# Early queries and keys in wide pieces, transposed head by head on TensorE, and strided values in four transfers per pair

## The chip, the cores and the metric

The kernel runs on one core of one Trainium2 chip. The metric is the device time of one execution in microseconds (us); lower is better. The core has five engines that work side by side and meet by semaphores: TensorE (PE; PEld is its loading of stationary tiles), VectorE (DVE), ScalarE (ACT), GpSimd (POOL) and SyncE (SP), which here only issues transfers. Each engine runs its own list of instructions strictly in order, so an instruction that waits holds up all that stand behind it. "SPq" and "ACTq" in the profile are the issue of transfers by SP and ACT.

## The reference

Eight batches of attention with 8 heads, 576 positions and 64 columns per head, followed by a gated feed-forward product of 4608 tokens. The first four heads see a local window of 32 positions, the other four only positions that are equal modulo 32.

```python
scores = scale * np.matmul(q, k.transpose(0, 1, 3, 2))
rel = pos[:, None] - pos[None, :]
mask_local = (rel >= 0) & (rel < stride)
mask_strided = (rel >= 0) & (pos[None, :] % stride == pos[:, None] % stride)
masks = np.stack([mask_local if h < H // 2 else mask_strided for h in range(H)], axis=0)
scores = np.where(masks[None, :, :, :], scores, -1000000000.0)
attn = softmax(scores)
x = np.matmul(attn, v).transpose(0, 2, 1, 3).reshape(B * S, H * D)
h = x @ w_in
g = h * np.clip(h + 3.0, 0.0, 6.0) / 6.0
out = g @ w_out
```

The softmax is written out in the reference (maximum, exponential, sum with 1e-9 added). All inputs are float32; `w_in` is 512 x 2048, `w_out` 2048 x 512.

## The kernel before

**Tiling.** Heads are worked in pairs, so a batch has four pairs: 0 and 1 are local, 2 and 3 strided. Pair numbers stand in the tile names (`qn_2` is the loaded query of a pair 2, `kn_2` its keys, `v_2` its values). The feed-forward part works on tiles of 512 tokens, one per batch, and on the 64 tokens that are left over of each batch, collected over four batches. A tile makes 16 chunks of `w_in` (`ph`, lines 969 to 971: three matmuls with split operands), gates them (`u` on ACT and DVE, `gh` on ACT, `gl` on POOL) and adds each chunk's product with `w_out` to `acc` (lines 927 to 929). Weights are loaded as raw words (`rawi`, `rawo`, line 287), taken apart on ACT, joined on DVE (`fi`, `fo`, line 303) and split into a high and a low part on ACT or POOL (lines 309 to 315). So DVE, ACT and POOL prepare weights and attention while PE multiplies.

**Pairs.** The first eight pairs (batches 0 and 1) go through `kept_pair`, the rest through `pair`. In `kept_pair` the four pairs of batch 0 are "early": their queries and keys come as rows with positions on the partitions (line 454, by SP, for the second pair to start by ACT's queue, two transfers per tensor), PE transposes them against an identity (line 461) into PSUM, and ACT or DVE copies the result to `qplain`, `kplain`, `qt` or `kt` (lines 473 and 475). The strided pairs of batch 1 are loaded by `load_qk` (line 360, four transfers) and transposed by DVE (line 492). Then come scores (`ps`, lines 551 and 554), the softmax in `e`, its transposition on DVE (`atloc` line 632, `atkept` line 637), the product with the values (`pv`, lines 379 and 689), and the high and low part of the result, `x` and `left` (lines 396 and 399), which the feed-forward tile reads. Strided values are loaded by line 511: for each of the two heads four transfers, one for each residue of the position modulo 4.

**Order.** Nothing is ordered by hand. `Plan.emit` is a list scheduler: each operation has an engine, an estimated time, a due time, what it reads and writes, and, for transfers, a time to land; the scheduler simulates the engines with these numbers and emits the instructions in the order that comes out. So a changed estimate can move instructions on every engine. Where PE would be idle ahead of the first products, the plan fills in matmuls of the identity (`idle`, line 1075), one per 0.22 us of planned idle time. Transfers of SP and ACT share eight semaphores in turn: each transfer waits until the one eight places earlier has landed.

Of the kernel before, what the change touches and what calls it, by code (L numbers as in the profile page):

```python
# [10 lines left out]
F32 = mybir.dt.float32  # L11
# [8 lines left out]
P = 128  # L20
# [145 lines left out]
def attention_ffn(ctx: ExitStack, tc, q, k, v, w_in, w_out, out):  # L166
# [241 lines left out]
    def kept_pair(g):  # L408
# [33 lines left out]
        for x in "qk":  # L442
# [6 lines left out]
            if early:  # L449

                def load(x=x, nkey=nkey):
                    t = new(wp, nkey, [P, NQB, 2, D], F32, f"{x}n{nm}")
                    for j in range(2):
                        (nc.scalar if g == 1 else nc.sync).dma_start(
                            t[:QB, :, j], {"q": q, "k": k}[x][b, h0 + j].rearrange("(i p) d -> p i d", p=QB))
                tb = [slot(early) for _ in range(2)]

                def tr(x=x, nkey=nkey, tb=tb):
                    ps = [psum(tb[h], f"{x}p{nm}{h}") for h in range(2)]
                    for i in range(NQB):  # L460
                        nc.tensor.transpose(ps[i // 3][:, i % 3 * QB:i % 3 * QB + QB],
                                            tiles[nkey][:QB, i].rearrange("p j d -> p (j d)"), tiles["ident",][:QB, :QB])

                def evac(e, x=x, tb=tb, h=0):
                    ps, to, half = tiles[tb[h].key][:, :S // 2], qk_of(x), NPOS // 2
                    if loc:
                        c0 = (PAD if x == "k" else 0) + S // 2 * h
                        to = to[:, c0:c0 + S // 2]
                    else:
                        to = to.rearrange("c (r m) -> c m r", r=STRIDE)[:, half * h:half * h + half]  # L470
                        ps = ps.rearrange("c (m r) -> c m r", r=STRIDE)
                    if e == "ACT":
                        nc.scalar.copy(to, ps)
                    else:
                        nc.vector.tensor_copy(to, ps)
                op("ACT" if g == 1 else "SP", 1.06, load, writes=[nkey], due=-60 + 2 * g + (x == "k") - 900 * (g == 1), after=0.9)
                op("PE", 0.13 * NQB * slow, tr, reads=[("ident",), nkey, "plain", tkey[x]], writes=tb, take=tb, due=due - 1020, mode="s")
                for h in range(2):
                    op({"ACT": 0.45, "DVE": 0.4} if loc else {"ACT": 0.65, "DVE": 0.65}, 0, partial(evac, h=h), reads=[tb[h]],
                       writes=[tkey[x]] if h == 0 else [tkey[x] + (1,) if isinstance(tkey[x], tuple) else tkey[x] + "1"], give=tb[h], due=due - 19)  # L480
                continue
# [4 lines left out]
            def tr(x=x, nkey=nkey):  # L486
# [3 lines left out]
                else:  # L490
                    to = to.rearrange("c (r m) -> c m r", r=STRIDE)[:, :NPOS]
                nc.vector.transpose(to, tiles[nkey])
# [11 lines left out]
        def load_v():  # L504
            if loc:
                load_windows(tiles[vkey], b, h0)
                return
            for j in range(2):
                rows = v[b, h0 + j].rearrange("(m t i) d -> i m t d", t=8, i=4)
                for i in range(4):  # L510
                    nc.sync.dma_start(tiles[vkey][PAD * i:PAD * i + NPOS, j], rows[i])  # L511
        op("SP", 1.6 if loc else 6.5, load_v, writes=[vkey], due=-48.8 if g == 1 else -54.5 + 2 * g if early else due - 30, early=0 if early else due - 35, after=1.3)


# [164 lines left out]
        else:  # L679
# [14 lines left out]
            for h in range(2):  # L694
# [3 lines left out]
                def place(x, h=h):  # L698
                    return x.rearrange("c (m t a) -> c t a m", t=8, a=4)[:, 4 * h:4 * h + 4]
                nown = TOK // STRIDE  # L700
# [408 lines left out]
```

## Time and profile before

| | |
|---|---|
| time, median of 3 runs | 948.95 us (948.93 to 950.05) |
| span of the profiled execution (its own time is recorded as this span) | 950.4 us |
| granted TensorE clock, mean | 0.987 |
| PE busy | 931.9 us, 98% |
| DVE, ACT, POOL busy | 578.0, 497.6, 440.8 us |
| HBM read, written | 46.73, 9.44 MB |

The span of the one profiled execution lies 1.45 us above the median of the timed runs. A row of the timeline reads: start, duration, engine, line, operation, tile written and tiles read, how many instructions are merged, and in brackets the idle time of the engine before it with the instruction that ended it. The granted clock is the share of TensorE's full clock that it was given; 0.50 is half pace.

### The profile page before, as it was taken

The numbers are of one execution on the slowest core, as the hardware profiler recorded it, in microseconds if no ns is written. First come the engines' busy times: TensorE is split into PE (matmuls) and PEld (weight loads), VectorE is DVE, ScalarE is ACT, GpSimd is POOL, SyncE is SP. The second block draws the span as 40 slices with busy tenths as digits, with TensorE's granted clock in tenths as the row PEclk, the third lists the DMA queues.
The fourth block names the chain that finished last, engine by engine and source line by source line (L and its number), as shares of the span: only waits on it lengthen the run. The fifth ranks groups of instructions, "written<-read, shape, count | busy, mean of one in ns | idle before, by whom it ended". The sixth has DMA issues, their size and how long they took to land.

```text
span 950.4 us, 15327 instructions
## 1 busy us (share of the span) xinstructions
PE 931.9 (98%) x5084; PEld 773.0 (81%) x5084; DVE 578.0 (61%) x1635; ACT 497.6 (52%) x1290; POOL 440.8 (46%) x437
## 2 busy tenths in 40 slices
PE   9979999999999999999999999999999999999997
PEld 8757787888888888988888888888887888888896
DVE  6876677778776766555576678786765775111111
ACT  5756857755565546455355555565554553322332
POOL 5656888554544444434444445444444452222221
PEclk9789999999999999999999999999999999999999
DMA  9658630432333123213113322232223200100000
GB/s 218 215 137 234 159 86 1 99 64 56 60 83 70 36 46 81 49 38 60 26 35 77 66 54 52 55 96 55 52 54 96 53 14 14 45 1 1 31 15 22
DMA packets 201031, 64.25 MB, mean 68 GB/s; under 512 B 189176, under 2 KB 189176, under 8 KB 200952
## 3 DMA queue, kind: packets, MB, share of 16 engines
q1 hardware_dynamic: 198584, 62.69, 29.0%
q10 hardware_dynamic: 2368, 0.59, 0.4%
q8 instruction: 40, 0.66, 0.3%
q14 instruction: 39, 0.32, 0.1%
HBM read 46.73 MB, written 9.44 MB: 59 GB/s over the span
## 4 chain that ended last, share of the span: by engine, by line
PE 88%; SPq 6%; DMA 3%; issue 1%; ACT 1%; DVE 0%; POOL 0%; ACTq 0%; POOLq 0%; DVEq 0%
PE acc L927 12%; PE acc L929 12%; PE ph L969 12%; PE acc L928 12%; PE ph L970 12%; PE ph L971 12%; PE ps L804 3%; SPq L511 2%; PE pv L379 2%; PE phl L969 2%; SPq L773 2%; DMA rawi<-in_moe_w_in_dram 2%; PE phl L971 1%; PE phl L970 1%; PE accl L929 1%; SPq L360 1%
## 5 line engine op out<-in xcount | busy, mean ns | idle before, releaser
L998 POOL TENSOR_TENSOR gl<-u,gh 128x512 fp32r<-128x512 f32 x128 | 169.4, 1323 | 276.6 <-ACT gh L993 253.3
L927 PE MATMUL acc<-wo,gh 128*128 128x512 f32 x512 | 203.0, 396 | 2.2 <-DVE u L985 2.2
L969 PE MATMUL ph<-x,wi 128*128 128x512 f32 x512 | 204.2, 399 | 0.0
L970 PE MATMUL ph<-x,wi 128*128 128x512 f32 x512 | 201.9, 394 | 0.2 <-DVE x L399 0.2
L971 PE MATMUL ph<-x,wi 128*128 128x512 f32 x512 | 201.6, 394 | 0.0
L929 PE MATMUL acc<-wo,gl 128*128 128x512 f32 x512 | 200.7, 392 | 0.0
L928 PE MATMUL acc<-wo,gh 128*128 128x512 f32 x512 | 200.4, 391 | 0.0
L981 ACT ACTIVATE u<-ph,three 128x512 f32<-128x512 f32 x128 | 88.2, 689 | 182.0 <-PE ph L971 181.5
L985 DVE SCALAR_TENSOR_TENSOR u<-u,ph 128x512 f32<-128x512 f32 x128 | 87.7, 686 | 142.3 <-ACT u L981 141.2
L828 ACT ACTIVATE e<-e,st 126x126 f32<-126x126 f32 (+2 forms) x264 | 102.7, 390 | 53.9 <-DVE st L822 53.4
L927 PEld LDWEIGHTS acc<-wo,gh 128*128 128x128 f32 x512 | 96.5, 188 | 22.3 <-DVE u L985 2.6
L971 PEld LDWEIGHTS ph<-x,wi 128*128 128x128 f32 x512 | 97.1, 190 | 20.9
L929 PEld LDWEIGHTS acc<-wo,gl 128*128 128x128 f32 x512 | 96.3, 188 | 21.0 <-POOL gl L998 0.2
L969 PEld LDWEIGHTS ph<-x,wi 128*128 128x128 f32 x512 | 97.1, 190 | 19.8 <-DVE u L985 0.4
L993 ACT CAST gh<-u 128x512 fp32r<-128x512 f32 x128 | 79.4, 621 | 62.1 <-DVE u L985 52.8
L970 PEld LDWEIGHTS ph<-x,wi 128*128 128x128 f32 x512 | 97.2, 190 | 17.2 <-DVE x L399 0.5
L928 PEld LDWEIGHTS acc<-wo,gh 128*128 128x128 f32 x512 | 96.5, 188 | 17.7
L844 POOL TENSOR_TENSOR e<-e,st 96x96 f32<-96x96 f32 (+1 forms) x72 | 71.0, 1000 | 82.1 <-DVE st L839 61.0
L822 DVE CUSTOM_DVE_ANT_0 e<-ps,e 126x126 f32<-126x126 f32 (+2 forms) x264 | 63.9, 278 | 2.2
L861 DVE STREAM_TRANSPOSE atstr<-e 32x160 f32<-32x160 f32 x168 | 56.3, 335 | 7.8 <-POOL e L844 4.8
L861 DVE STREAM_TRANSPOSE atloc<-e 32x192 f32<-32x192 f32 (+1 forms) x144 | 52.2, 363 | 13.1 <-POOL e L844 10.4
L804 PEld LDWEIGHTS ps<-ksplit,qq 128*96 128x96 f32 (+1 forms) x264 | 43.6, 173 | 12.4 <-issue 1.6
(133 smaller groups left out, 1394.6 us busy)
## 6 DMA issues: line engine op xcount, KB each, us to landing
rawi<-in_moe_w_in_dram SPq DMA_DIRECT2D x16, 512.0 KB
rawo<-in_moe_w_out_dram SPq DMA_DIRECT2D x16, 512.0 KB
out_dram<-ob SPq DMA_DIRECT2D x32, 256.0 KB
qn<-in_q_dram SPq DMA_DIRECT2D x112, 72.0 KB
kn<-in_k_dram SPq DMA_DIRECT2D x112, 72.0 KB
ksplit<-ksplit SPq DMA_DIRECT2D x48, 144.0 KB
vt<-in_v_dram SPq DMA_DIRECT2D x24, 160.0 KB
vt<-in_v_dram SPq DMA_DIRECT2D x120, 31.5 KB
```

The source lines that it names most:

```text
L828: nc.scalar.activation(e, e, AF.Exp, bias=st_of(j, 0)[:, i:i + 1], scale=-1.0, accum_out=st_of(j, 1)[:, i:i + 1])
L861: nc.vector.transpose(at[ks, i0:, qs], e[qs, i0:, ks])
L927: nc.tensor.matmul(acc, gh, woh, start=fc == 0, stop=False)
L928: nc.tensor.matmul(acc, gh, wol, start=False, stop=False)
L929: nc.tensor.matmul(acc, gl, woh, start=False, stop=end)
L969: nc.tensor.matmul(ph, wih, xh, start=n_ == 0, stop=False)
L970: nc.tensor.matmul(ph, wih, xl, start=False, stop=False)
L971: nc.tensor.matmul(ph, wil, xh, start=False, stop=n_ == NCC - 1)
L981: nc.scalar.activation(u, tiles[pk][:, :n], AF.Relu, bias=three)
L985: nc.vector.scalar_tensor_tensor(out=u, in0=u, scalar=6.0, in1=tiles[pk][:, :n], op0=ALU.min, op1=ALU.mult)
L993: nc.scalar.copy(g, tiles[uk][:, :n])
L998: eng.tensor_tensor(out=g, in0=tiles[uk][:, :n], in1=tiles[gk[0]][:, :n].bitcast(F32), op=ALU.subtract)
```

## The change

Three things are altered, all of them in `kept_pair`.

1. An early query or key tensor comes in one transfer for both heads instead of two. On a partition lie neighbouring positions, 6 for a local pair (96 partitions, 1.5 KB per head) and 8 for a strided pair (72 partitions, 2 KB per head), where before each position and head was a piece of 256 B.
2. PE transposes each head by itself, as a plain matmul with the piece of 64 columns as the stationary tile and the identity moving, 12 for a local tensor and 16 for a strided one, where there were 6 transpositions of both heads together. The copies out of PSUM put the positions back in order.
3. Strided positions are ordered differently inside the 32 residues: residue 8a + t in place of 4t + a. One transfer then takes, for both heads, runs of 8 positions (2 KB) for one a, so the strided values of all kept pairs need four transfers instead of eight. The DVE transposes of batch 1 and the places where `x` is written follow the new order.

The plan's estimates go with it: 0.55 instead of 1.06 for an early load, 2.1 instead of 6.5 for the strided values, and 0.13 per piece on PE.

```diff
-                def load(x=x, nkey=nkey):
-                    t = new(wp, nkey, [P, NQB, 2, D], F32, f"{x}n{nm}")
-                    for j in range(2):
-                        (nc.scalar if g == 1 else nc.sync).dma_start(
-                            t[:QB, :, j], {"q": q, "k": k}[x][b, h0 + j].rearrange("(i p) d -> p i d", p=QB))
+                rows, ni = (QB, NQB) if loc else (S // 8, 8)
+
+                def load(x=x, nkey=nkey, rows=rows, ni=ni):
+                    t = new(wp, nkey, [P, 2, ni * D], F32, f"{x}n{nm}")
+                    (nc.scalar if g == 1 else nc.sync).dma_start(
+                        t[:rows], {"q": q, "k": k}[x][b, h0:h0 + 2].rearrange("j (p i) d -> p j (i d)", i=ni))
...
-                    for i in range(NQB):
-                        nc.tensor.transpose(ps[i // 3][:, i % 3 * QB:i % 3 * QB + QB],
-                                            tiles[nkey][:QB, i].rearrange("p j d -> p (j d)"), tiles["ident",][:QB, :QB])
+                    half = ni // 2
+                    for i in range(ni):
+                        for j in range(2):
+                            nc.tensor.matmul(ps[i // half][D * j:D * j + D, i % half * rows:i % half * rows + rows],
+                                             tiles[nkey][:rows, j, D * i:D * i + D], tiles["ident",][:rows, :rows],
+                                             start=True, stop=True)
...
-                        c0 = (PAD if x == "k" else 0) + S // 2 * h
-                        to = to[:, c0:c0 + S // 2]
+                        c0, half = PAD if x == "k" else 0, NQB // 2
+                        to = to[:, c0:c0 + S].rearrange("c (p i) -> c i p", i=NQB)[:, half * h:half * h + half]
+                        ps = ps.rearrange("c (i p) -> c i p", i=half)
                     else:
-                        to = to.rearrange("c (r m) -> c m r", r=STRIDE)[:, half * h:half * h + half]
-                        ps = ps.rearrange("c (m r) -> c m r", r=STRIDE)
+                        to = to.rearrange("c (t a m) -> c t a m", t=8, a=4)[:, 4 * h:4 * h + 4, :, :NPOS]
+                        ps = ps.rearrange("c (t m a) -> c t a m", t=4, a=4)
...
-                op("ACT" if g == 1 else "SP", 1.06, load, writes=[nkey], due=-60 + 2 * g + (x == "k") - 900 * (g == 1), after=0.9)
-                op("PE", 0.13 * NQB * slow, tr, reads=[("ident",), nkey, "plain", tkey[x]], writes=tb, take=tb, due=due - 1020, mode="s")
+                op("ACT" if g == 1 else "SP", 0.55, load, writes=[nkey], due=-60 + 2 * g + (x == "k") - 900 * (g == 1), after=1.0)
+                op("PE", 0.13 * ni * slow, tr, reads=[("ident",), nkey, "plain", tkey[x]], writes=tb, take=tb, due=due - 1020, mode="s")
...
-                    to = to.rearrange("c (r m) -> c m r", r=STRIDE)[:, :NPOS]
+                    to = to.rearrange("c (t a m) -> c m a t", t=8, a=4)[:, :NPOS]
...
-            for j in range(2):
-                rows = v[b, h0 + j].rearrange("(m t i) d -> i m t d", t=8, i=4)
-                for i in range(4):
-                    nc.sync.dma_start(tiles[vkey][PAD * i:PAD * i + NPOS, j], rows[i])
-        op("SP", 1.6 if loc else 6.5, load_v, writes=[vkey], due=-48.8 if g == 1 else -54.5 + 2 * g if early else due - 30, early=0 if early else due - 35, after=1.3)
+            rows = v[b, h0:h0 + 2].rearrange("j (m a t) d -> a m j (t d)", a=4, t=8)
+            for a in range(4):
+                nc.sync.dma_start(tiles[vkey][PAD * a:PAD * a + NPOS].rearrange("p j t d -> p j (t d)"), rows[a])
+        op("SP", 1.6 if loc else 2.1, load_v, writes=[vkey], due=-48.8 if g == 1 else -54.5 + 2 * g if early else due - 30, early=0 if early else due - 35, after=1.3)
...
-                    return x.rearrange("c (m t a) -> c t a m", t=8, a=4)[:, 4 * h:4 * h + 4]
+                    return x.rearrange("c (m a t) -> c t a m", t=8, a=4)[:, 4 * h:4 * h + 4]
```

The plan orders the instructions anew. The start of PE's list, before and after (`qp` and `kp` are the transposed queries and keys in PSUM, `ps_000` the first scores; a row's end is the shape and how many):

```order
L1075 MATMUL idle<-ident 128x128 x14
L461 MATMUL qp_00_178<-ident,qn_0_97 128x96 x3
L461 MATMUL qp_01_179<-ident,qn_0_97 128x96 x3
L461 MATMUL qp_20_198<-ident,qn_2_100 128x96 x3
L461 MATMUL qp_21_199<-ident,qn_2_100 128x96 x3
L461 MATMUL kp_00_219<-ident,kn_0_147 128x96 x3
L461 MATMUL kp_01_220<-ident,kn_0_147 128x96 x3
L461 MATMUL kp_20_234<-ident,kn_2_150 128x96 x3
L461 MATMUL kp_21_235<-ident,kn_2_150 128x96 x3
L551 MATMUL ps_000_247<-kplain,qplain 96x128 x4
```

And after the change:

```order
L1079 MATMUL idle<-ident 128x128 x15
L464 MATMUL qp_00_176<-ident,qn_0_97 64x96 x6
L464 MATMUL qp_01_177<-ident,qn_0_97 64x96 x6
L464 MATMUL qp_20_203<-ident,qn_2_99 64x72 x8
L464 MATMUL qp_21_204<-ident,qn_2_99 64x72 x8
L464 MATMUL kp_00_237<-ident,kn_0_105 64x96 x6
L464 MATMUL kp_01_238<-ident,kn_0_105 64x96 x6
L464 MATMUL kp_20_261<-ident,kn_2_107 64x72 x8
L464 MATMUL kp_21_262<-ident,kn_2_107 64x72 x8
L555 MATMUL ps_000_279<-kplain,qplain 96x128 x4
```

The order is the same; one more idle matmul stands in front, and 56 matmuls stand where 24 transpositions stood.

SP's list, behind the ten weight transfers that end batch 0's loads, before (the names with `_2` and `_3` are the strided pairs of batch 1 here):

```order
L287 DMA rawo_551<-in_moe_w_out_dram 128x1024
L360 DMA qn_2_559<-in_q_dram 32x18x32 x4
L360 DMA kn_2_586<-in_k_dram 32x18x32 x4
L511 DMA v_2_539<-in_v_dram 18x8x64 x8
L360 DMA qn_3_701<-in_q_dram 32x18x32 x4
L511 DMA v_3_768<-in_v_dram 18x8x64 x8
L360 DMA kn_3_852<-in_k_dram 32x18x32 x4
L287 DMA rawi_876<-in_moe_w_in_dram 128x1024
```

And after:

```order
L287 DMA rawo_430<-in_moe_w_out_dram 128x1024
L360 DMA qn_2_441<-in_q_dram 32x18x32 x4
L360 DMA kn_2_482<-in_k_dram 32x18x32 x4
L515 DMA v_2_598<-in_v_dram 18x2x512 x4
L360 DMA qn_3_735<-in_q_dram 32x18x32 x4
L360 DMA kn_3_835<-in_k_dram 32x18x32 x4
L515 DMA v_3_812<-in_v_dram 18x2x512 x4
L287 DMA rawi_891<-in_moe_w_in_dram 128x1024
```

The values take four transfers each, and the keys of pair 3 stand ahead of its values. Farther up in the same list, the first group of strided values is parted: `v_2` now stands ahead of the first six weight transfers and `v_3` behind them, where both stood behind them.

DVE's list where the feed-forward product waits for the last two pairs of batch 0 (`x_11` and `x_31` are the low parts of the results of pairs 1 and 3, `qt_2` the transposed query of batch 1), before:

```order
L399 TENSOR_TENSOR x_11_771<-pv_10_745,x_10_770 128x512
L399 TENSOR_TENSOR left_1_81<-pv_11_746,left_1_80 128x64
L492 STREAM_TRANSPOSE qt_2_384<-qn_2_559 128x18x32
L637 STREAM_TRANSPOSE atkept<-e_108 32x8x32 x4
L492 STREAM_TRANSPOSE kplain<-kn_2_586 128x18x32
L303 SCALAR_TENSOR_TENSOR fo_738<-fo_738,rawo_471 128x512
L399 TENSOR_TENSOR x_31_833<-pv_30_774,x_30_832 128x16x16
L399 TENSOR_TENSOR left_3_85<-pv_30_774,left_3_84 128x16x2
```

And after:

```order
L497 STREAM_TRANSPOSE qt_2_466<-qn_2_441 128x18x4x8
L399 TENSOR_TENSOR x_11_827<-pv_10_789,x_10_826 128x512
L399 TENSOR_TENSOR left_1_81<-pv_11_790,left_1_80 128x64
L641 STREAM_TRANSPOSE atkept<-e_110 32x8x32 x4
L497 STREAM_TRANSPOSE kplain<-kn_2_482 128x18x4x8
L303 SCALAR_TENSOR_TENSOR fo_753<-fo_753,rawo_305 128x512
L303 SCALAR_TENSOR_TENSOR fo_779<-fo_779,rawo_355 128x512
L399 TENSOR_TENSOR x_31_873<-pv_30_816,x_30_872 128x4x4x16
```

`qt_2` has moved ahead of `x_11`, and a second `fo` ahead of `x_31`. Behind the opening the lists of all engines differ in many places in how attention, weights and feed-forward products are interleaved; the last 60 rows of PE's list are the same.

More of the change, by code (lines that the diff above doesn't have):

```diff
@@ L456, in kept_pair, with tr @@
                 tb = [slot(early) for _ in range(2)]
-                def tr(x=x, nkey=nkey, tb=tb):
+                def tr(x=x, nkey=nkey, tb=tb, rows=rows, ni=ni):
                     ps = [psum(tb[h], f"{x}p{nm}{h}") for h in range(2)]
-                    for i in range(NQB):
-                        nc.tensor.transpose(ps[i // 3][:, i % 3 * QB:i % 3 * QB + QB],
-                                            tiles[nkey][:QB, i].rearrange("p j d -> p (j d)"), tiles["ident",][:QB, :QB])
+                    half = ni // 2
[4 more added lines that the diff above has]
+                                             start=True, stop=True)
@@ L464, in evac @@
                 def evac(e, x=x, tb=tb, h=0):
-                    ps, to, half = tiles[tb[h].key][:, :S // 2], qk_of(x), NPOS // 2
+                    ps, to = tiles[tb[h].key][:, :S // 2], qk_of(x)
                     if loc:
-                        c0 = (PAD if x == "k" else 0) + S // 2 * h
-                        to = to[:, c0:c0 + S // 2]
-                    else:
-                        to = to.rearrange("c (r m) -> c m r", r=STRIDE)[:, half * h:half * h + half]
-                        ps = ps.rearrange("c (m r) -> c m r", r=STRIDE)
+                        c0, half = PAD if x == "k" else 0, NQB // 2
+                        to = to[:, c0:c0 + S].rearrange("c (p i) -> c i p", i=NQB)[:, half * h:half * h + half]
+                        ps = ps.rearrange("c (i p) -> c i p", i=half)
+                    else:
+                        to = to.rearrange("c (t a m) -> c t a m", t=8, a=4)[:, 4 * h:4 * h + 4, :, :NPOS]
+                        ps = ps.rearrange("c (t m a) -> c t a m", t=4, a=4)
```

## The prediction

> **What bounds the kernel now.** I read the head of the page first, then the windows table, for how busy TensorE (PE) is in each stretch.
>
> ```profile
> span 950.4 us, 15327 instructions
> ...
> 80.00:200.00 120.00, 120.00 (x646) 96.47 (x645) 86.38 (x194) 85.06 (x195) 89.02 (x91) 0.99 0.44 107
> 200.00:400.00 200.00, 200.00 (x1120) 167.28 (x1119) 142.56 (x441) 112.07 (x308) 93.28 (x82) 1.00 0.27 57
> ```
>
> After the stretch come PE's busy time, then PEld, DVE, ACT and POOL, the granted clock, the DMA share and GB/s. From 80 us on PE is busy 120.00 of 120 and 200.00 of 200 us, so nothing that the other engines do there can shorten the run. What can be won lies ahead of 80 us, and whatever PE gains there moves the whole rest forward, if weights and attention keep up. Next I cut the opening into windows of about 3.4 us, the spacing at which the clock column changes.
>
> ```profile
> 31.50:34.90 3.40, 2.55 (x22) 2.24 (x23) 3.33 (x9) 2.20 (x9) 3.16 (x5) 0.98 0.20 46
> 34.90:38.30 3.40, 3.40 (x23) 3.13 (x23) 3.37 (x6) 2.71 (x10) 2.58 (x4) 0.50 0.28 58
> ...
> 58.70:62.10 3.40, 1.60 (x20) 1.49 (x20) 3.37 (x7) 2.15 (x6) 1.03 (x2) 1.00 0.19 43
> 62.10:65.50 3.40, 2.43 (x13) 2.23 (x11) 2.92 (x5) 1.70 (x7) 3.32 (x3) 0.50 0.47 86
> 65.50:68.90 3.40, 3.40 (x13) 2.52 (x12) 1.51 (x2) 1.53 (x5) 2.44 (x3) 0.50 0.36 68
> 68.90:72.30 3.40, 3.40 (x10) 2.45 (x9) 0.37 (x1) 2.15 (x6) 1.43 (x2) 0.50 0.19 43
> ...
> 75.90:79.30 3.40, 1.20 (x5) 0.68 (x4) 2.78 (x5) 1.18 (x2) 0.51 (x1) 0.98 0.92 323
> 79.30:82.70 3.40, 3.40 (x10) 2.63 (x9) 1.38 (x2) 2.38 (x6) 1.55 (x3) 0.52 1.02 401
> ```
>
> There are two losses: idle PE (1.60 of 3.40 busy at 58.7, 1.20 of 3.40 at 75.9), and behind each badly filled window a granted clock of 0.50, for three windows from 62.1 and one from 79.3. The timeline of PE gives its pauses from 57 us on, with their releasers.
>
> ```profile
> 59.17 1.22 PE L689 MATMUL pv<-atkept,v 128*64 128x72 f32 x16 [2.07 <-DVE atkept L637]
> 61.71 1.60 PE L554 MATMUL ps<-kplain,qt 64*128 64x72 f32 x8 [1.33 <-DVE left L399]
> 64.27 1.98 PE L554 MATMUL ps<-kplain,qt 64*128 64x72 f32 x8 [0.97 <-ACT e L568]
> 78.71 0.50 PE L927 MATMUL acc<-wo,gh 128*128 128x512 f32 x1 [2.20 <-DVE u L985]
> ```
>
> They sum to 2.07 + 1.33 + 0.97 + 2.20 = 6.6 us, and PE mostly waits for VectorE (DVE). Why DVE is late stands in its own rows.
>
> ```profile
> 56.33 1.19 DVE L492 STREAM_TRANSPOSE qt<-qn 128x576 f32<-128x576 f32 x1 [1.94 <-DMA qn<-in_q_dram]
> ...
> 60.25 0.68 DVE L303 SCALAR_TENSOR_TENSOR fo<-fo,rawo 128x512 int32<-128x512 int32 x1
> ...
> 66.86 1.19 DVE L492 STREAM_TRANSPOSE qt<-qn 128x576 f32<-128x576 f32 x1 [1.84 <-DMA qn<-in_q_dram]
> ...
> 76.28 1.26 DVE L492 STREAM_TRANSPOSE kt<-kn 128x576 f32<-128x576 f32 x1 [7.01 <-DMA kn<-in_k_dram]
> ```
>
> DVE works in order. Three times a transpose of the second batch's queries or keys stands at its head and waits for a load, 1.94, 1.84 and 7.01 us, with `atkept`, `x` and `u`, which PE needs, queued behind it. The loads are late because their queue, SP's, is:
>
> ```profile
> 20.98 15.86 SPq L511 DMA_DIRECT2D v<-in_v_dram  x16
> 36.89 0.94 SPq L287 DMA_DIRECT2D rawo<-in_moe_w_out_dram  x2
> ...
> 43.83 9.18 SPq L360 DMA_DIRECT2D qn<-in_q_dram  x4
> ...
> 56.49 6.45 SPq L511 DMA_DIRECT2D v<-in_v_dram  x8
> ...
> 65.20 6.87 SPq L511 DMA_DIRECT2D v<-in_v_dram  x8
> 72.17 2.03 SPq L360 DMA_DIRECT2D kn<-in_k_dram  x4
> ```
>
> The first sixteen strided value transfers hold SP for 15.86 us, 0.8 each. So ten weight transfers start at 36.89 instead of about 21, the `qn` behind them is issued from 43.83 to 53.0 as they drain, and sixteen more value transfers (13.3 us) stand ahead of `kn`, issued only at 72.17.
>
> **The change part by part.** *The loads.* 32 value issues become 16. If one keeps its price of 0.8 us, the first group takes 6.4 instead of 15.86; if it falls to that of a weight issue (0.94 for two), 3.8. I take the dearer end: SP is 9.5 us earlier behind the first group, and 6.7 us more behind the second (13.3 halved). The bytes gain too:
>
> ```profile
> DMA packets 8410, 2.09 MB, mean 199 GB/s; under 512 B 8410, under 2 KB 8410, under 8 KB 8410
> ...
> DMA packets 1400, 4.68 MB, mean 390 GB/s; under 512 B 264, under 2 KB 264, under 8 KB 1399
> ```
>
> The first row is 2.5 to 13 us, all packets of 256 B; the second is 40 to 52 us, mostly weights in rows of 4 KB. Packets of 1.5 and 2 KB lie between 199 and 390 GB/s, and I take the nearer, 390. The early queries and keys are 16 x 144 KB = 2.36 MB: 11.9 us at 199, 6.1 at 390, so the weights behind them gain some 6 us on top. `qn` then lands 9 to 15 us ahead of 56.3, where 1.94 would be enough. The last `kn` uses the buffer of the first `qn` and is issued when `qt_2` is done, near 55.6; with its 2.03 us of issue and as much to land it is there by 60, while its turn on DVE came at 69.3 (76.28 - 7.01). So all three DVE waits go.
>
> *PE's pauses and clock.* With the waits go the four pauses, **-6.6 us**, and the two badly filled windows that stand ahead of the half clock. Under it PE was busy 2.43 + 3.40 + 3.40 + 3.40 = 12.6 us, work of 6.3 us at the full clock: **-6.3 us**.
>
> The windows in which the clock changes are 3.4 us apart (34.9, 62.1, 72.3, 79.3). The Trainium skill, "TensorE: Matmul & The Clock Gate", Part 1, has a free-running window of that length and says that a window of idleness drops the clock to half; the trace agrees with the length. By that rule no window of the changed kernel is idle enough to drop it, which is the forecast; but the row at 31.50 shows a drop behind a window that was busy 2.55 of 3.40, and this gives the second case below.
>
> *The front.* Each transposition of [96, 128] becomes two plain matmuls with 64 columns; the strided tensors are cut in 8 pieces of 72 rows.
>
> ```profile
> 1.36 6.30 PE L1075 MATMUL idle<-ident 128*128 128x128 f32 x28 [1.36 <-POOL ident masks.py:199]
> 7.50 1.16 PE L461 MATMUL qp<-ident,qn 96*128 96x96 f32 x12
> 8.82 1.55 PE L461 MATMUL kp<-ident,kn 96*128 96x96 f32 x12 [0.16 <-DMA kn<-in_k_dram]
> ...
> 9.54 0.40 ACT L473 COPY kplain<-kp 128x288 f32<-128x288 f32 x1 [0.43 <-PE kp L461]
> ...
> 10.29 1.63 PE L551 MATMUL ps<-kplain,qplain 64*96 64x128 f32 x16
> 10.40 0.69 ACT L473 COPY kplain<-kp 128x288 f32<-128x288 f32 x1 [0.46 <-PE kp L461]
> ...
> 27.64 1.14 PEld L379 LDWEIGHTS pv<-atloc,v 128*64 128x64 f32 x28
> ...
> 30.16 1.07 PEld L689 LDWEIGHTS pv<-atkept,v 128*64 128x64 f32 x16 [0.15 <-issue]
> ...
> 35.91 1.97 PEld L689 LDWEIGHTS pv<-atkept,v 128*64 128x64 f32 x16
> ```
>
> PE waits for no query load here: the idle matmuls end just as it starts at 7.50, so faster loads win only the 0.16 at 8.82. A transposition is one record, a plain f32 matmul two (L379 shows 28 for 14). The four tensors of the first two pairs had 24 records in 10.29 - 7.50 = 2.8 us; now they have 2 x (12 + 16 + 12 + 16) = 112. A record's price lies between 41 ns (L379, 1.14 / 28, halves of the columns in turn), 67 ns (L689, one half all the time) and 123 ns (L689 at the half clock). The new ones alternate halves, so I take 41: 4.6 us, 1.8 more; and one more idle matmul, two records of 6.1 / 28 = 0.22, adds 0.4. **+2.2 us** before the first scores, and as ScalarE (ACT) follows them nearly without a pause I let it all through. Such stationary tiles were 64 columns before, so I see no reason for less than 41 on 96 columns; 72 columns could cost three quarters of it, which bounds the front from below at some +1.6 (64 of 112 records at 31 ns: 0.6 less).
>
> *What is late next.* DVE's list has `qt_2` (1.19) ahead of `x_11` now, and a second `fo` (0.68) ahead of `x_31`: **+1.9**, up to PE, which waits for both. And `gl_0` on POOL (L998) comes behind several weight parts of its length:
>
> ```profile
> L998 POOL TENSOR_TENSOR gl<-u,gh 128x512 fp32r<-128x512 f32 x128 | 169.4, 1323 | 276.6 <-ACT gh L993 253.3
> ```
>
> What PE would wait for it no row shows: between nothing and two such subtractions, 2.6 us. I take a middle value, **+1.5**, as the rows are near neither end.
>
> *At nothing.* The evacuations trade places: local ones, contiguous, are now strided, and the strided ones, contiguous. With 0.40 and 0.69 us for the two forms sixteen copies could gain or lose 0.3 each, 8 of either sign. Strided writes of `x`, and DVE's transposes into the new row order, move as many elements as before; if they were a quarter dearer, 4 transposes of 1.2 us would cost 1.2 in all, hidden where DVE no longer waits. `atstr` moves from POOL to DVE, which had waited there.
>
> **The sum.** -6.6 - 6.3 + 2.2 + 1.9 + 1.5 = **-7.3 us**, from the profiled 950.4 to 943.1. The profile has only the span; it lies 1.45 us above the median of the runs, 948.95, which I take as what the profiled execution adds: 948.95 - 7.3 = **941.7 us**.
>
> **The rivals.** *The clock drops again.* The remaining pauses (1.9 us and more, small matmuls between them) leave a window near 60 us filled like the one at 31.50; for it speaks that row, against it that the window before the drop at 62.1 was emptier still, 1.60 of 3.40, and its 2.07 and 1.33 us pauses go. Half of 2.43 + 3.40 + 3.40 comes back, 4.6: 946.3.
>
> *Little is left of it.* The records cost 67 ns on top: 112 x 0.026 = 2.9 more. Then 949.2, no change. For it speaks that PE may wait for each load of weights as in L689; against it the turns between halves.
>
> *Slower.* The first transposes meet a PE that is still at its slow pace: the idle records last 0.22 each there. At 123 ns the 112 records need 13.8 us, 11.0 more than before instead of 1.8, and pairs 1 and 3 pass the same on to ACT where it waits for `kp` (some 2 us): 941.7 + 9.2 + 2 = 952.9. It decides from the record price at which front and residue eat the 12.9: (2.8 + 12.9 - 0.4 - 3.4) / 112 = 106 ns. Against it: the records of L551 at 10.29, as wide as the idle ones, take 1.63 / 16, 102 ns, so by then PE was past its slow pace.
>
> **How the numbers follow.** Forecast 0.47, clock drops again 0.27, little left 0.13, slower 0.13. A measurement of this kernel tells some 0.2%, 1.9 us, from no change. Faster by over that: 0.47 + 0.27 = 0.74; within: 0.13; slower: 0.13. The low end is the forecast with a front of +1.6 and nothing late on POOL, 939.6, and some 1 us for the evacuations, 938.5; the high end takes in the second and third case, 949.5. That leaves 0.13 above and some 0.05 below.
>
> **What would show it.** Right: the value issues take under 7 us in the first group; no DVE wait for `qn` or `kn` over 0.5 us; PE's first scores start near 12.5; granted clock 1.00 from 50 us on; PE full from about 72 instead of 80. Wrong: scores later than 15 us (record price), 0.50 in the clock column between 60 and 75 (second case), or new pauses of PE behind 80 us, for `gl` or weights, which would mean that the front engines and not SP set the opening.

## The result, and the profile after

The changed kernel takes 957.25 us (median of 4 runs, 954.82 to 958.62) where the kernel before, on the same chip, takes 949.5 (948.93 to 950.46): a ratio of 1.0075 (95% interval 1.0055 to 1.0095). It is **slower by 0.75%**, some 7.7 us, where 941.7 was forecast. Two later repeats of both kernels gave ratios of 1.0037 (1.0022 to 1.0051) and 1.0053 (1.0036 to 1.0071).

The profiled execution after has a span of 953.0 us and took 954.82, so a run's time lies 1.8 us above its span. By the same offset the profiled 950.4 of before would be a run of some 952, one of its slower ones; the two spans therefore show less of a difference than the runs do, and a gain counted against before's trace comes out some 2.6 us larger than one counted against its median.

First the opening. This is the list of PE's waits between 40 and 100 us, before and then after; the columns are the waiting instruction, what ended the wait, the sum in us, how often, and the longest.

```profile
PE pv L689 <- DVE atkept L637: 2.8, 2, 2.1
PE acc L927 <- DVE u L985: 2.2, 1, 2.2
PE ps L554 <- DVE left L399: 1.3, 1, 1.3
PE ps L554 <- ACT e L568: 1.0, 1, 1.0
PE pv L379 <- DVE atloc L632: 0.9, 1, 0.9
PE ph L970 <- DVE x L399: 0.2, 1, 0.2
```

```profile
PE pv L379 <- DVE atloc L636: 2.5, 1, 2.5
PE ph L974 <- DVE x L399: 1.5, 2, 1.0
PE pv L693 <- DVE atkept L641: 0.8, 1, 0.8
PE ps L558 <- DVE left L399: 0.3, 1, 0.3
```

The sums are 8.4 and 5.1 us. DVE no longer waits for a load: its four transposes of the second batch's queries and keys, in the timeline of DVE after, carry no bracket, which is where an idle time would stand.

```profile
52.28 1.20 DVE L497 STREAM_TRANSPOSE qt<-qn 128x576 f32<-128x576 f32 x1
55.86 1.30 DVE L497 STREAM_TRANSPOSE kplain<-kn 128x576 f32<-128x576 f32 x1
62.25 1.19 DVE L497 STREAM_TRANSPOSE qt<-qn 128x576 f32<-128x576 f32 x1
63.88 1.23 DVE L497 STREAM_TRANSPOSE kt<-kn 128x576 f32<-128x576 f32 x1
```

The reason is on SP's queue, where the value issues of the first group now take 2.63 + 3.94 = 6.6 us instead of 15.86, and each later one 1.45 instead of 6.45 and 6.87:

```profile
11.59 2.63 SPq L515 DMA_DIRECT2D v<-in_v_dram  x4
...
19.02 3.94 SPq L515 DMA_DIRECT2D v<-in_v_dram  x4
...
46.38 1.45 SPq L515 DMA_DIRECT2D v<-in_v_dram  x4
...
55.54 1.45 SPq L515 DMA_DIRECT2D v<-in_v_dram  x4
```

The front, in the timeline of PE: the first scores (L555) start at 10.69 us, where they started at 10.29, and the 112 records between 6.39 and 10.69 cost 38 ns each. (In a later trace of the same kernel, x10 below, the idle matmuls last until 7.54 and the first scores start at 11.85, at the same 38 ns.)

```profile
1.37 5.09 PE L1079 MATMUL idle<-ident 128*128 128x128 f32 x30 [1.37 <-POOL ident masks.py:199]
6.39 2.21 PE L464 MATMUL qp<-ident,qn 96*64 96x96 f32 x56
8.43 2.31 PE L464 MATMUL kp<-ident,kn 96*64 96x96 f32 x56
10.69 1.61 PE L555 MATMUL ps<-kplain,qplain 64*96 64x128 f32 x16
```

Then the part that was taken as settled. These are the windows of after that stand beside the two of before from 80 us on; the first figure behind the stretch is PE's busy time.

```profile
80.00:200.00 120.00, 116.08 (x623) 91.65 (x622) 80.52 (x175) 80.63 (x181) 86.62 (x89) 1.00 0.31 76
200.00:400.00 200.00, 198.94 (x1110) 164.88 (x1106) 147.51 (x459) 111.78 (x317) 95.17 (x84) 1.00 0.29 61
```

PE was busy 120.00 of 120 there and is now 116.08. The timeline of PE names the pauses:

```profile
151.33 0.50 PE L975 MATMUL ph<-x,wi 128*128 128x512 f32 x1 [1.51 <-POOL wi L315]
153.74 0.50 PE L973 MATMUL ph<-x,wi 128*128 128x512 f32 x1 [1.21 <-DVE u L989]
177.47 0.44 PE L808 MATMUL ps<-ksplit,qq 128*96 128x256 f32 x2 [0.22 <-POOL qq L757]
178.86 0.50 PE L973 MATMUL ph<-x,wi 128*128 128x512 f32 x1 [0.94 <-DVE u L989]
```

To see where time is won and lost I numbered PE's 3648 feed-forward matmuls (`ph` and `acc`) in each trace and compared the starts of equal numbers, as these are the same work in the same place of the computation. The first column is before's start in us, the others are differences from it:

| feed-forward matmul | before | after | after, repeated (x3) | new data, old lists (x1) | old data, new lists (x2) |
|---|---|---|---|---|---|
| 60 | 79.8 | -6.4 | -10.4 | -2.8 | +0.2 |
| 180 | 118.8 | -6.8 | -10.8 | -4.1 | -0.3 |
| 300 | 153.7 | -5.8 | -9.8 | -4.1 | +0.7 |
| 420 | 183.8 | -1.4 | -5.3 | -4.1 | +8.0 |
| 1020 | 337.6 | +2.5 | -1.4 | -4.1 | +11.8 |
| 3647 (last) | 944.9 | +2.4 | -1.6 | -3.9 | +11.7 |

The opening gains 6.4 us against before's trace, close to the 7.3 of the forecast, and more than that is given back between 150 and 340 us. The gain in the two executions of the changed kernel differs by 4.0 us; what they give back from matmul 180 on is the same, 9.2. A third trace (x10) is 9.8 us ahead at 180 and gives back 10.7; behind the pauses at 150 us it has half the clock for a while (0.66 from 150 to 155 us). Lists that differ take attention work a little earlier or later between two numbers, so single differences between 420 and the last are good to a microsecond or two; the last one is exact.

Pauses between matmuls understate the loss, as PE also starts more slowly behind each: the next record behind the one at 151.33 starts 0.34 us later, where 0.23 is usual. If for each pair of neighbouring PE records one adds up what exceeds the usual distance of its kind, behind 85 us, after has **8.0 us more** than before, 4.8 of it between 100 and 200. The rest up to 9.2 I can't place.

### The profile page after: what moved, and what is told of

Its sections match the earlier page's. It is cut to its first block, busy times and chain, and to the rows that moved or that the text cites. A ratio compares the mean times of both kernels' runs of the same rounds, so it can differ in the third digit from the quotient of the medians.

```text
span 953.0 us, 15645 instructions
## 1 busy us (share of the span) xinstructions
PE 933.9 (98%) x5258; PEld 769.8 (81%) x5258; DVE 581.8 (61%) x1634; ACT 499.3 (52%) x1291; POOL 441.3 (46%) x437
## 4 chain that ended last, share of the span: by engine, by line
PE 85%; DVE 8%; ACT 2%; issue 2%; POOL 1%; SPq 1%; DMA 1%; POOLq 0%; DVEq 0%; ACTq 0%
PE acc L931 12%; PE acc L933 11%; PE acc L932 11%; PE ph L973 11%; PE ph L974 11%; PE ph L975 11%; PE ps L808 3%; PE pv L379 2%; PE phl L973 1%; PE phl L975 1%; PE phl L974 1%; PE accl L933 1%; PE pv L883 1%; PE accl L931 1%; PE accl L932 1%
## 5 line engine op out<-in xcount | busy, mean ns | idle before, releaser
L832 ACT ACTIVATE e<-e,st 96x128 f32<-96x128 f32 (+2 forms) x264 | 102.8, 391 | 68.0 <-DVE st L826 67.5
L848 POOL TENSOR_TENSOR e<-e,st 96x96 f32<-96x96 f32 (+1 forms) x72 | 68.8, 968 | 76.6 <-DVE st L843 59.1
L826 DVE CUSTOM_DVE_ANT_0 e<-ps,e 96x128 f32<-96x128 f32 (+2 forms) x264 | 64.5, 279 | 2.6
L399 DVE TENSOR_TENSOR x<-pv,x 128x512 fp32r<-128x512 f32 (+3 forms) x48 | 31.6, 658 | 43.0 <-ACT x L396 25.3
```

Of the source, the lines that this page charges most:

```text
L832: nc.scalar.activation(e, e, AF.Exp, bias=st_of(j, 0)[:, i:i + 1], scale=-1.0, accum_out=st_of(j, 1)[:, i:i + 1])
```

## The experiments

Three theories were open. **A, the lists**: the gain is real, but the plan, with three changed estimates, writes other lists for all engines (of the 1436 operations that the plan gives PE, 1060 stand in another place), and these lists make PE wait. **B, the data**: the new forms (strided writes of `x`, the new row order) cost it later. **C, the supply**: weights and gates come no faster than before, so what PE gains ahead of 80 us it must wait away.

### Lists and data apart

x1 has all of the change but its estimates, so the plan writes the lists of before, with not an operation of any engine in another place:

```diff
-op("SP", 0.55, load, ... after=1.0)
+op("SP", 1.06, load, ... after=0.9)
-op("PE", 0.13 * ni * slow, tr, ...
+op("PE", 0.13 * NQB * slow, tr, ...
-op("SP", 1.6 if loc else 2.1, load_v, ...
+op("SP", 1.6 if loc else 6.5, load_v, ...
```

> The changed kernel's loads, transposes and value layout, with the planner given the durations of before (1.06, 0.9, 0.13 x 6, 6.5), so that all five engines keep the lists of before but for the replaced rows (POOL: not a row differs). Theory A (the opening's gain of 6.4 us is real, and the later lists that the new durations make cost it): 943 us, pauses of PE behind 85 us as in before, about 1 us in 100 to 200. Theory B (the new data path itself costs it later: strided writes of x, new row order): 955 to 958, pauses as in the changed kernel. Theory C (no list can give more than before's weights and gates do; what PE gains ahead of 80 us it waits away behind): 949 to 951, with PE pauses for weights or u of 5 to 6 us between 100 and 200.

x2 is the reverse, the kernel before with the three new estimates:

```diff
-op("SP", 1.06, load, ... after=0.9)
+op("SP", 0.55, load, ... after=1.0)
-op("PE", 0.13 * NQB * slow, tr, ...
+op("PE", 0.13 * (NQB if loc else 8) * slow, tr, ...
-op("SP", 1.6 if loc else 6.5, load_v, ...
+op("SP", 1.6 if loc else 2.1, load_v, ...
```

> The loads, transposes and value layout of before, with the planner given the new durations, so that the lists are those of the changed kernel but for the replaced rows. Theory A: the opening is as late as before's or later (PE full from 80 us), and the new lists still pause PE, though less as PE is later: 951 to 958. Theory B: as before, 948 to 951. Theory C: as before, 948 to 951, since PE is not early enough to wait.

x3 is the changed kernel on the same chip, and x4 the kernel before with `T0 = 44.1` instead of 44.0, which alters nothing but the lists.

> The changed kernel once more, beside the others on one chip: all theories 955 to 958.5, ratio to before 1.0055 to 1.0095, with 4 to 7 us of PE pauses between 100 and 200.

> The kernel before with the planner's start time T0 at 44.1 instead of 44.0: the same work and data path, but three quarters of PE's list and most of the other lists stand in another order. Theory A: another order alone moves the time by several us, most likely up (before's order is one of many): 950 to 957. Theories B and C: within 2 us of before, 947.5 to 951.5.

| kernel | us, median | ratio to before (949.63 us, 19 runs) |
|---|---|---|
| x1, new data, old lists | 947.02 | 0.9966 (0.9954 to 0.9978) |
| x3, new data, new lists | 953.31 | 1.0037 (1.0022 to 1.0051) |
| x2, old data, new lists | 961.80 | 1.0111 (1.0081 to 1.0140) |
| x4, old data, another list | 962.44 | 1.0143 (1.0127 to 1.0159) |

Where the expectations named a figure for A (943 us for x1, 951 to 958 for x2, 955 to 958.5 for x3, 950 to 957 for x4), the median lies outside it; what bears A out is the pattern. The new lists cost 953.31 - 947.02 = 6.3 us with the new data and 961.80 - 949.63 = 12.2 with the old; the new data gain 2.6 in the old lists and 8.5 in the new, part of the 8.5 being clock (x2's runs were granted 0.938 to 0.988, x3's 0.993 to 0.999). One row of the windows shows it, 100 to 200 us, of before, x1, x2 and x4 in turn:

```profile
100.00:200.00 100.00, 100.00 (x542) 80.50 (x540) 71.14 (x166) 69.94 (x164) 72.92 (x75) 1.00 0.36 80
```

```profile
100.00:200.00 100.00, 100.00 (x556) 80.75 (x557) 72.08 (x170) 68.38 (x157) 73.12 (x75) 1.00 0.31 72
```

```profile
100.00:200.00 100.00, 96.11 (x495) 75.67 (x494) 62.69 (x140) 67.28 (x150) 69.19 (x75) 0.97 0.26 64
```

```profile
100.00:200.00 100.00, 97.15 (x512) 77.07 (x512) 61.59 (x135) 65.57 (x149) 66.97 (x71) 1.00 0.30 67
```

PE is full with before's lists, whatever the data, and waits with the new ones, whatever the data. For x4 this row holds only a small part of the loss: counted by equal matmuls, x4 is 3.9 us behind before at 420 and 13.2 at the last, and some 6 of these come from one pause with half the clock behind it (0.98 from 200 to 300 us), which no row here explains ("issue" is a wait for nothing that the profile shows):

```profile
287.17 0.45 PE L804 MATMUL ps<-ksplit,qq 128*96 128x256 f32 x2 [2.83 <-issue]
```

B falls: x1 has all the new forms and no new pause. C falls too: in x1 PE is 4.1 us early and keeps it to the end, and in x2 PE is not early at all and waits all the same, for the same weight and the same gate as after:

```profile
PE ph L969 <- DVE u L985: 2.0, 2, 1.2
PE ph L971 <- POOL wi L315: 1.5, 1, 1.5
PE ps L804 <- DMA ksplit<-ksplit: 0.4, 1, 0.4
```

(x2's waits of PE between 100 and 200 us.) Behind x2's pauses the clock is at half for a while, 0.97 in its row above, and that takes some 3 of its 12 us. A stands, with a gain in the old lists smaller than the 6.4 it took over: 4.1 in the trace, 2.6 in the runs.

### Which part of the data brings the gain

x5 keeps before's lists and before's queries and keys, and takes of the change only the values and the row order that comes with them:

```diff
-for j in range(2):
-    rows = v[b, h0 + j].rearrange("(m t i) d -> i m t d", t=8, i=4)
-    for i in range(4):
-        nc.sync.dma_start(tiles[vkey][PAD * i:PAD * i + NPOS, j], rows[i])
+rows = v[b, h0:h0 + 2].rearrange("j (m a t) d -> a m j (t d)", a=4, t=8)
+for a in range(4):
+    nc.sync.dma_start(tiles[vkey][PAD * a:PAD * a + NPOS].rearrange("p j t d -> p j (t d)"), rows[a])
```

> The lists of before; of the change only the values in four transfers per pair and the row order they bring; queries and keys as before. If the value issues were what held the opening up (the step of the prediction): all of the gain of the new data path in the old lists, 946 to 948, ratio near 0.9966, no wait of DVE for qn or kn over 0.5 us. If the larger pieces of queries and keys carry it: 949 to 950, ratio 0.999 to 1.001.

946.50 us against 950.21 of before, ratio 0.9966 (0.9950 to 0.9982): all of what x1 has, and no wait of DVE for a load ahead of 100 us. So the values, and the SP time that their issues free, are the gain in these lists. Wide loads of queries and keys with transposes head by head add nothing that can be measured in these lists.

### Can the pause be mended where it stands?

In the changed kernel's timelines the last weight part of the fourth group reaches PE late because its rows stand, on ACT, behind two groups of copies of scores that wait for PE, and on POOL behind subtractions of scores. x6 takes the changed kernel and moves this part's rows ahead, six rows in all, PE's and SP's lists untouched. This is what moves on ACT and POOL, shapes left out (on DVE the join `fi` moves past one maximum):

```diff
 ACT
+ACTIVATE fi<-rawi
+ACTIVATE rawi<-rawi
 COPY e<-ps_104
 COPY e<-ps_110
-ACTIVATE fi<-rawi
-ACTIVATE rawi<-rawi
 ACTIVATE e<-e
 POOL
+TENSOR_TENSOR wi<-fi,wi
+CAST wi<-fi
 TENSOR_TENSOR e<-e,mband
 MEMSET e
 TENSOR_TENSOR wi<-fi,wi
 TENSOR_TENSOR e<-e,st_1
-CAST wi<-fi
 TENSOR_TENSOR e<-e,st_1
-TENSOR_TENSOR wi<-fi,wi
```

> The changed kernel with the preparation of the last part of the first weight's fourth group moved ahead in the lists of ACT (2 rows), DVE (1) and POOL (3, with the subtraction of the part before it), past copies, masks and subtractions of attention scores; PE's and SP's lists are untouched. Theory A (the place in the list makes the wait): the pause of 1.7 us at 145 to 149 goes and the one of 1.4 behind it shrinks, 1.7 to 3.1 us less than the changed kernel, ratio 1.001 to 1.005 where the changed kernel had 1.0037 and 1.0075. Theory D (the engines have no time left there, whatever the order): the pauses move a few us on and keep their sum, ratio as the changed kernel's.

960.22 us, ratio 1.0111 (1.0094 to 1.0128): slower than the changed kernel, and theory A in the form "one row stands badly" is wrong. (Part of the difference is clock: x6's five runs were granted 0.988 or 0.989, and the changed kernel's runs at 0.988 to 0.990 took 957.03 to 958.62.) The wait for the weight is gone, and a longer one for the gate `u` stands in its place. DVE's timeline of x6 says why:

```profile
153.85 2.28 DVE L638 STREAM_TRANSPOSE atloc<-e 32x192 f32<-32x192 f32 x6 [1.01 <-POOL e L617]
156.16 0.69 DVE L305 SCALAR_TENSOR_TENSOR fo<-fo,rawo 128x512 int32<-128x512 int32 x1
156.77 1.28 DVE L991 SCALAR_TENSOR_TENSOR u<-u,ph 128x512 f32<-128x512 f32 x2
```

And the timeline of PE has the wait that came of it:

```profile
157.51 0.53 PE L975 MATMUL ph<-x,wi 128*128 128x512 f32 x1 [3.72 <-DVE u L991]
```

The two gates stand behind six transposes, which wait for POOL, and a weight join. The first pause of the changed kernel hid most of the second, and behind the longer one the clock falls for a few us, 0.81 and 0.62 in the windows 156 to 159 and 159 to 162 us. x9 moves these gates, and their relus on ACT, ahead as well; x10 is the changed kernel beside it.

```diff
 DVE
-STREAM_TRANSPOSE atloc<-e
-SCALAR_TENSOR_TENSOR fo<-fo,rawo
 SCALAR_TENSOR_TENSOR u_12<-u_12,ph_12
 SCALAR_TENSOR_TENSOR u_13<-u_13,ph_13
+STREAM_TRANSPOSE atloc<-e
 TENSOR_REDUCE st_1<-e
+SCALAR_TENSOR_TENSOR fo<-fo,rawo
```

> The weight part moved ahead as in x6_one_weight_ahead, and beside it the two gates that PE waited 3.72 us for there: on DVE both u stand ahead of six transposes of attention weights and of a weight join, on ACT both relus ahead of two weight rows. Theory A (the list's place makes the wait, and the two waits lay over each other): at 150 to 155 a pause of at most 0.9 us instead of 3.9, no half clock behind it, 2 to 3 us faster than the changed kernel on the same chip and 3 to 6 faster than x6, ratio to before 0.999 to 1.005. Theory D (the chain of attention through POOL, ACT and DVE has no time left, so PE waits a little later for something else): new pauses of 2 us or more between 155 and 200, no faster than the changed kernel.

> The changed kernel on the same chip, for the row above: ratio to before 1.0037 to 1.0075 by all theories; pauses of 1.7 and 1.4 us at 145 to 154 as in both its traces.

x9 954.79 us, ratio 1.0075 (1.0048 to 1.0103); x10 954.83, ratio 1.0053 (1.0036 to 1.0071). No gain again; PE's waits between 140 and 200 us in x9 are now

```profile
PE ph L975 <- DVE u L991: 1.7, 2, 0.8
PE acc L933 <- POOL wo L313: 1.4, 1, 1.4
PE acc L934 <- POOL wo L317: 0.8, 1, 0.8
PE acc L935 <- POOL gl L1004: 0.7, 1, 0.7
PE ps L810 <- POOL qq L759: 0.3, 1, 0.3
```

which is the pause passed on to the next weights and the next gate; from matmul 180 to the last x9 gives back 12.3 us. So theory D of these expectations (no time is left there, whatever the order) fits these two tries, with the rest of the new lists as it was: what was put ahead made the next thing late. The work isn't too much for the engines, since before's lists do the same work there without a wait. That the new lists come to this point with more left to do is a reading that one count fits. The windows view for line 315 alone, POOL's last step on each of the 32 weight parts, counts them (the figure behind x) up to PE's feed-forward matmuls 180 and 240; in after

```profile
0.00:112.00 112.00, 26.15 (x19) 0.95 0.74 205
0.00:128.60 128.60, 31.68 (x23) 0.96 0.71 191
```

and in before

```profile
0.00:118.80 118.80, 28.47 (x21) 0.90 0.76 193
0.00:135.10 135.10, 32.37 (x24) 0.91 0.71 180
```

At equal progress of PE the new lists have two parts fewer ready, then one. x2 has the same 19 and 23 although its PE is 6.5 us later than after's, x1 the 21 and 24 of before although its PE is 4.1 us earlier: the count belongs to the lists, not to the speed. That it makes the waits is not shown.

### Weights earlier in all lists

x8 gives each weight part of the changed kernel a due time 4 us earlier and lets the plan write the lists anew:

```diff
-due = T0 + fc * TILE / NFC - 5.0 + 0.01 * k
+due = T0 + fc * TILE / NFC - 9.0 + 0.01 * k
```

> The changed kernel with the planner's due time of each weight part 4 us earlier (9.0 instead of 5.0 ahead), which makes it plan all later lists anew. Theory A: fewer waits for weights between 100 and 200, 2 to 4 us faster than the changed kernel, ratio 0.998 to 1.003; a due time does not govern the other rows, so other pauses may come. Theory D: no faster than the changed kernel, ratio 1.003 to 1.010.

947.86 us, ratio 0.9986 (0.9967 to 1.0004): most of the loss is gone, by one number of the plan. PE is busy 99.47 of 100 us between 100 and 200, with one wait of 0.5 for `u`; from matmul 180 to the last its trace still gives back 3.5 us. Its interval holds 1, so it is as fast as before and not shown to be faster.

### The new front with the old rest

x7 runs the plan twice, with the new and with the old estimates, and takes the rows that start ahead of 60 us in the new plan, with all they need, from the one, and the rest from the other:

```diff
+first, keys1, _ = self.simulate(False)
+rest, keys2, _ = self.simulate(True)
+head, todo = set(), [n for t, _, n, e in first if n is not None and t < 60.0]
...
+merged = [(n, e, keys1) for _, _, n, e in first if n is None or n in head]
+merged += [(n, e, keys2) for _, _, n, e in rest if n is not None and n not in head]
```

> The data path of the change. The rows that the changed kernel's plan starts ahead of 60 us, and what they need, stand as in the changed kernel's lists; all others stand as in before's. Theory A: the opening of the changed kernel (6.4 to 10.4 us ahead of before at 80 us) and the few pauses of before behind it: 940 to 944, ratio 0.990 to 0.995. Theory C in its weak form (before's lists allow only so much lead): about as the new data path in the old lists, 946 to 948, with new pauses of 2 to 6 us in 100 to 200.

945.41 us against 950.21, ratio 0.9958 (0.9940 to 0.9976), **the fastest of all, 0.4% ahead of before** and, by the ratios of one chip each, 0.8 to 1.2% ahead of the changed kernel. Between 100 and 200 us PE is busy 100.00 and keeps its lead, so the weak form of C is out as well, for a lead of 3.8 us; no trace has a larger lead with these lists. It missed the 940 to 944 by 1.4 us: in its trace, of a run of 948.99, the opening is only 3.8 us ahead at matmul 180, as three stretches of half clock stand in it (the first is shown below). The run with the highest granted clock, 0.997, took 942.36. Its interval overlaps those of x1 and x5, so the new front is not shown to add anything to the values alone.

### Which lists cost, and which do not

x11 is the kernel before with `T0 = 43.9`, x12 is x5 with the true time for the values:

```diff
-T0 = 44.0
+T0 = 43.9
```

```diff
-op("SP", 1.6 if loc else 6.5, load_v, ...
+op("SP", 1.6 if loc else 2.1, load_v, ...
```

> The kernel before with T0 at 43.9: again the same work in other lists, but here a quarter of PE's rows move and the lists up to PE's 899th row stay; where the planner lays the weight parts against PE's feed-forward products, they are as early as in before. Theory A in its narrow form (not another order as such costs, but one that has weight parts fewer ready at the same product of PE): within 0.3% of before, 948 to 952, 21 weight parts ready at PE's 180th feed-forward matmul and 24 at its 240th. Theory A in its wide form (before's order is a lucky one, any other costs): 955 or more, as x4_other_order.

> Values in four transfers alone, as x5_values_only, but the planner told of it (2.1 instead of 6.5 us for a pair's values); queries, keys and their durations as before. If the planner's number for the values is what makes the bad lists: fewer than 21 and 24 weight parts at PE's 180th and 240th feed-forward matmul, PE pauses between 100 and 200, and 3 to 6 us more than x5, ratio 1.000 to 1.003. If only the new numbers for queries and keys did: as x5, ratio 0.995 to 0.998.

x11: 951.11 us against 949.98, ratio 1.0015 (1.0004 to 1.0025), PE busy 100.00 of 100 and the 21 and 24 weight parts of before: another list need not cost, and the wide form of A is out. (x11's lists are close to before's, as its expectation says.) x12: 952.83, ratio 1.0025 (1.0008 to 1.0042), so the true estimate for the values alone takes back what the values had won, as expected. But the reason given for it failed: x12 has 22 and 25 weight parts ready, more than before, and PE waits nevertheless, for gates:

```profile
PE ph L968 <- DVE u L984: 1.7, 2, 1.3
```

x4, with 21 and 24, waits as well. So the count of weights goes with the changed kernel and x2, and is no general mark of a bad list.

## Why the prediction was wrong, point by point

**What bounds the opening: right.** The value issues take 6.6 us in the first group (under 7 was asked for), no wait of DVE for `qn` or `kn` is left, and PE is full from some 65 us where 72 was forecast. x5 shows that the values alone bring the gain in before's lists. One price under it was off: packets moved at 241 GB/s from 2.5 to 13 us, where the nearer row's 390 was taken.

**The sum of the opening: near in the traces, by luck, as its terms were each off.** Forecast -7.3; measured -6.4 at matmul 60 in the first trace, -10.4 and -9.3 in the repeats, all against before's trace. That trace is of a run some 2.6 us above the median; the 1.45 us between its span and the median, taken as what the profiled execution adds, were too small a measure of it, as a run's time lies 1.8 above its span. An estimate from medians: if every run gives back 9.2, the opening gained 1.5 us in the first comparison (957.25 - 949.5 = 7.7), 5.5 and 4.5 in the two repeats. PE's waits fell by 3.3 us (8.4 to 5.1), not by 6.6 less 1.9: the four named ones shrank from 6.6 to 0.3, but `atloc` grew from 0.9 to 2.5 and `x` from 0.2 to 1.5, 2.9 where +1.9 was put down. The front cost +0.4 instead of +2.2, as PE's idle matmuls ended 1.1 us sooner in this execution; in x10 they didn't, and it cost 1.6. The record price of 41 ns held at 38, so the slow rival (106 ns and more) was far off. No wait for `gl` came there, so the +1.5 was nothing.

**The clock: both cases are true.** The two executions of one kernel read, from 60 to 70 us, first trace and x3:

```profile
60.00:70.00 10.00, 9.58 (x37) 6.85 (x35) 6.48 (x9) 6.27 (x19) 6.06 (x6) 0.66 0.93 266
```

```profile
60.00:70.00 10.00, 10.00 (x53) 7.82 (x53) 7.03 (x13) 9.16 (x27) 9.07 (x10) 1.00 0.99 271
```

With the same lists one had the half clock there (and for a while from 50 to 60 us, 0.83) and the other had none; they are 4.0 us apart at matmul 60, close to the 4.6 at which that rival was priced. It was treated as a property of the kernel and differs from execution to execution. The kernel has a part in it: over the whole span the runs of before that the ratios rest on were granted 0.982 to 0.990, and the changed kernel's 0.988 to 0.999. The term also counted too little: before's clock is at 0.50 from 34.9 to 45.1 us too, and all three traces of the changed kernel read 1.00 from 30 to 45. From 10 to 85 us the clock is 0.84 in before and 0.93, 1.00 and 0.98 in the three, which is 7 to 12 us of full pace (an estimate: 75 us times the difference) and would be all of the gain that these traces show; x5, with 0.84 like before, has its 4.5 us at matmul 180 without it.

**The step that failed** is the first paragraph's: "nothing that the other engines do there can shorten the run. What can be won lies ahead of 80 us, and whatever PE gains there moves the whole rest forward, if weights and attention keep up." A full PE says that the lists of before feed it in time. It was read as if the lists behind 80 us stayed what they were, and the changed estimates had rewritten them, which was known. The condition at the end of the sentence got no price and no rival; its failure came up only among the signs that would make the forecast wrong ("new pauses of PE behind 80 us, for `gl` or weights"), and that is the sign that came. It could have been seen ahead: the start times that the plan computes while it writes the lists, estimates and no measurement, already hold pauses of PE at this place with the changed numbers, and in x4 and x12, and none in before or x11. By them PE's last operation ends at 932.7 us with before's numbers and at 940.1 with the changed ones, although the new estimates for the values are the shorter ones; the same figure is 932.8 for x11, 935.6 for x8, 936.3 for x12 and 944.0 for x4, which is the order of the measured ratios among the kernels with the old data and among those with the new (a ranking of six lists, found after the results). Priced by the runs, the step is 6.3 us (x3 less x1) with the new data, against an opening that is worth 2.6 in the old lists; the traces, counted from matmul 180 on and so without the opening's clock, put it at 9.2.

That is not all of the 15.6 us between 941.7 and 957.25. The changed kernel has 24 runs, in three comparisons. The six at a granted clock of 0.999 took 950.78 to 951.33 us, some 9 above the forecast, which is what the traces give back behind the opening; the eight at 0.988 to 0.990 took 957.03 to 958.62. So some 9 us go with the lists, and the 6 more that the first comparison has go with the clock, the rival that had been given 0.27; where in those runs the half clock stood no trace shows.

**The chance of a slower kernel**, 0.13, was given to one mechanism, the price of the transposes, in the part of the kernel that the change was about. The loss came where the change had no line at all.

What stays open: why one set of lists leaves PE waiting and another does not. The weights fit it for the changed kernel; x12 and x4 wait for gates and for `x`, and moving single rows mended nothing. It also stays open why the new front, 3 to 7 us better than the old one (x1) in the traces of the changed kernel, shows so little of it in x7. The clock goes with it: from 10 to 85 us it is 0.86 in the traces of x7 and of x1, and 0.93 to 1.00 in those of the changed kernel. Why x7, with the same rows of PE there, gets less is not shown.

## What to carry to other kernels

Where estimates or due times feed a scheduler, a change to them is a change to every list behind them: price the order apart from the work, by building the new work with the old numbers and the old work with the new ones (here -0.34% and +1.11%). A bottleneck engine that is 100% busy is proof only for the lists that were profiled, and it can still be starved by others; here the end that the scheduler computes for its own lists, 940.1 against 932.7 us, would have told it ahead of any run. A more truthful estimate need not give better lists, and lists that happened to be good are worth keeping when the work beneath them changes.

## What the runs showed of the hardware

The half clock can come behind a full stretch too. In x7, in windows of 1 us, PE is busy 1.00 of 1.00 from 16 us on, with small tiles, and the granted clock falls to 0.50 at 21 us for about 7 us:

```profile
19.00:20.00 1.00, 1.00 (x23) 0.93 (x24) 0.46 (x1) 0.92 (x5) 1.00 (x2) 1.00 0.88 258
20.00:21.00 1.00, 1.00 (x26) 0.92 (x20) 0.77 (x2) 0.94 (x5) 0.45 (x1) 1.00 1.05 414
21.00:22.00 1.00, 1.00 (x12) 1.00 (x10) 0.76 (x3) 0.77 (x2) 0.00 (x0) 0.54 0.99 401
22.00:23.00 1.00, 1.00 (x8) 0.87 (x6) 0.88 (x5) 0.82 (x4) 0.00 (x0) 0.50 1.03 397
```

All three traces of the changed kernel, with the same rows of PE there, show 1.00 from 19 to 28 us. The Trainium skill, "TensorE: Matmul & The Clock Gate", Part 1, says that the clock falls after a window of idleness; these rows don't show an idle one, unless small tiles count as partly idle, which no run here tells apart. Nor did a full stretch bring the full clock back at once: in the prediction's rows before stays at 0.50 from 65.5 to 72.3 us with PE busy 3.40 of 3.40. So the opening of this kernel is worth a different time from one execution to the next: x7's runs lie between 942.36 and 949.37 us, and differences of 1 or 2 us between kernels can be told only from many runs.
